# Two chained mixtures of experts after a dynamic convolution: one-hot rows built one group ahead, logits' steps with precedence in the order, and late second-layer weights for experts 4 to 7

## The chip, the cores and the metric

One core of one Trainium2 chip runs the whole program in one launch. The metric is the device time in microseconds (us). The engines are called as in the profile: PE (TensorE) multiplies matrices, PEld is its loading of stationary operands, DVE (VectorE) and ACT (ScalarE) work on whole tiles, POOL (GpSimd) issues the indirect transfers that gather and scatter rows, and SP (SyncE) issues all other DMAs and transposes from one queue. "The clock" is the TensorE clock that was granted, as a share of full speed: 1.00 is 2.4 GHz, 0.50 is 1.2 GHz.

## The reference

```python
# 7168 tokens of 192 numbers; 8 heads, 7 taps
w   = softmax(weight_gen, axis=-1)                       # per token and head
x   = einsum('bshk,bskhg->bshg', w, shifted(x_pad))      # dynamic convolution
# layer 1: 8 experts, 192 -> 1024 -> 192, two of them per token
l   = x @ w_gate + log1p(exp(x @ w_noise)) * noise
x   = sum over the 2 best experts e of l:  p_e * (relu(x @ w1[e]) @ w2[e])
# layer 2: 8 experts of the same size, one of them per token
l   = x @ w_gate2
x   = softmax(l)[best] * (relu(x @ w1b[best]) @ w2b[best])
```

What matters here is that a token's second-layer expert is known only when its first-layer output is complete, and that the rows must be sorted by expert before the big products start.

## The kernel before, in words

**Work and stages.** Tokens are handled in columns of 128, 56 columns in all. The first layer treats the columns in two groups: group 1 (columns j 0 to 17 of each half of the sequence) and group 2 (j 18 to 27). The products with the experts run in five phases, one after the other: phase 0 and phase 1 are the first layer on the early and the late columns of group 1, phase 2 is the first layer on group 2, phase 3 the second layer on group 1's tokens, and phase 4 the second layer on group 2's tokens. In a phase the sorted rows are cut into blocks of 128 rows with one expert each; two blocks with one expert make a double unit, else a block is a single unit. The first units of a phase have a fixed expert and read its weights from the resident tile `wres`; the singles that follow them may have any expert, and a copy `w` of the expert's weights is fetched for each of them by a DMA from SP, by ACT or by DVE (tuple `FE`, line 29).

**Products.** Weights and hidden values are kept as two f16 parts. `ph` is the first product of an expert, `hh` the rounded relu of it (ACT), `hl` the remainder (DVE, 128x512), `py` the second product. A step of a unit is ten matmuls of 256 columns (double) or twenty of 128 columns (single) into `ph`, followed by `py` matmuls of the unit before. Below, positions in a phase are counted in **pieces**: one piece is ten `ph` matmuls, so a step of a double unit is one piece and a step of a single unit two. A phase has 88 to 112 pieces; by count from the program's start, phase 3 holds pieces 288 to 376 and phase 4 pieces 376 to 464.

**A route** (`route_`, from line 1001) stands at the door of every phase. It is a chain: the logits of the last rows (`turn_thread`, line 647, has SP transpose the rows to `xtg`; `logit_thread`, line 668, multiplies them with the gate weights into `pm` and DVE writes `lg`), the choice of expert (`choose` or `settle`), ranks and places on DVE (`msk`, `blkh` and more), then one-hot rows on DVE in groups of `OG` = 8 columns (line 74): a one-hot of the place in the block (`pex`, from a comparison of `ipx` with the places) and one of the block (`bex`, comparison and multiplication by a code). PE multiplies each group's `pex` with `bex` into `pr` (lines 1191 to 1205), and from the sum DVE makes the table `src`. With `src`, POOL gathers rows (`gt<-rows,src`, `load_x`, line 1412), SP transposes them (`xt<-gt`, `turn_x`, line 1426) and `ph` of the next phase can begin.

**Between the layers.** POOL scatters first-layer outputs to `ybuf`. `combine_lane` (line 867) reads the two outputs of a token back (`rows<-ybuf`, `yl<-ybuf`, both on SP), sums them with the gates, splits the sum (`split_rows`), stores it (`store`, SP: `rows<-rows`) and puts it into the queue of `turn_thread`. `weight_lane` (line 463) loads raw weights of an expert and one of its two matrices (SP: `w<-in_moe_w_dram`; k=0 is the first matrix, k=1 the second), splits them on ACT and DVE and puts them into `wres`; for the second layer it starts with phase 2 (`replace_weights`, line 1551), and a matrix is written over the first layer's as soon as the last unit that needs the old one has been issued (`passed`).

**What sets the order.** All of this is written as Python generators, and the order of instructions on every engine is fixed when the program is built. `Feed` (line 211) holds the generators. Each says by `yield` on which engine its next instructions stand and which tiles they need (`yield None`: not now); `Clock` estimates when these would be ready. `pump`, called between the steps of the main loop (from line 1655), takes again and again the generator with the least time plus its `late` number, among those that are ready when PE would be free, so a lower `late` is a precedence. At a phase boundary whose route is not done, the rest of the route is issued without regard to PE (`until`). The second transpose of a four-column item, the logits and a `finish` thread (the end of a convolution item, started in `conv_lane`, line 762) are each such steps.

Each instruction is recorded from one helper, so all rows of the profile show one line, L189 (in the changed program L191).

```python
            for a in range(0, n, TPN):                 # turn_thread, TPN = 2
                ...
                xt = rt.tile([P, 4 * TPN, P], F16, name="xtg", bufs=XR)[:, 0:4 * k]
                yield "S", rows, xt
                SP.dma_start_transpose(xt, ...)
```

Of the kernel before, what the change touches and what calls it, by code (L numbers as in the profile page):

```python
# [16 lines left out]
P = 128  # L17
# [22 lines left out]
NC2 = 3  # L40
C2LATE = 0.0
R2LATE = -4.0
LLATE = 0.0
RLATE = -4.0
R0LATE = 2.0
XB = 1
TAPS = (2, 2, 2, 1)
# [2 lines left out]
HM = 1  # L50
WL2 = 2.0
EB = 2
TPN = 2
XR = 3
HT = 2
# [216 lines left out]
def moe_kernel(ctx: ExitStack, tc: tile.TileContext, x: bass.AP, wgen: bass.AP,  # L272
# [4 lines left out]
    V, A, G, PE, SP = [Eng(e, k, clk) for e, k in (  # L277
        (nc.vector, "V"), (nc.scalar, "A"), (nc.gpsimd, "G"), (nc.tensor, "P"), (nc.sync, "S"))]
    feed = Feed(clk)
# [8 lines left out]
    B, S, _ = x.shape  # L288
# [109 lines left out]
    wdone = [0, 0]  # L398
    have = [[[], []], [[], []]]
    started, pe_users, hurried = [], [], []  # L400
    passed = set()
    inv12 = [const.tile([P, E], F32, name=f"inv12_{m}") for m in range(2)]

# [59 lines left out]
    def weight_lane(m, tag, pieces, ln):  # L463
# [3 lines left out]
        def queue_of():  # L467

            return ("G", G) if m == 0 and not started and GQ else ("S", SP)

        def load(e, k):
            raw = wbuf.tile([P, 2 * QW], F16, name=tag, bufs=2).bitcast(F32)
            while m == 0 and (not loaded or hurried and not started):
                yield None
            q = queue_of()
            yield q[0], raw
            q = q[1]
            if k == 0:
                q.dma_start(raw[:, 0:F], wa[e, 0:P, :])
                q.dma_start(raw[0:64, F:QW], wa[e, P:D, 0:F // 2])  # L480
                q.dma_start(raw[64:P, F:QW], wa[e, P:D, F // 2:F])
            else:
                q.dma_start(raw.rearrange("p (f d) -> p f d", f=FT), wb[e].rearrange("(f p) d -> p f d", p=P))
            return raw
# [162 lines left out]
    def turn_thread():  # L647

        while True:
            if not queue:  # L650
                yield None
                continue
            r, ln, rows, t0, n = queue.pop(0)
            xts = []
            for a in range(0, n, TPN):
                k = min(TPN, n - a)
                while len(turned) >= XR:
                    yield None
                turned.append(1)
                xt = rt.tile([P, 4 * TPN, P], F16, name="xtg", bufs=XR)[:, 0:4 * k]  # L660
                yield "S", rows, xt
                SP.dma_start_transpose(xt, rows.bitcast(F16)[:, a:a + k].rearrange("p t c -> p (t c)"))
                xts += [xt[:, 4 * v:4 * v + 4] for v in range(k)]
            pending[ln] = False
            lqueue.append((r, t0, n, xts))
            yield ()
# [95 lines left out]
    def conv_lane(items, early, pool, ln):  # L762
# [39 lines left out]
        busy = []  # L802
        while cur:
# [56 lines left out]
            if q and (XB == 1 or ln):  # L860
                nxt = yield from load(*q)
            busy.append(1)
            feed.add(finish(r, acc, t0, n, busy, on_pe + (ln > 0), t), lane_th[ln][2])
            cur = q


    def combine_lane(r, pool, ln, idxs):
# [4 lines left out]
        while idxs:  # L872
# [9 lines left out]
            for c, o in ((1, z), (0, y)):  # L882
                k = 0
                while k < n:
                    t, v = at[b, ja + k], 1
                    while k + v < n and at[b, ja + k + v] == t + v:
                        v += 1
                    SP.dma_start(o[:, k:k + v], bass.AP(tensor=yb.tensor, offset=yb.offset + (2 * t + c) * P * D,
                                                        ap=[[D, P], [2 * P * D, v], [1, D]]))
                    k += v  # L890
            yield "A", z
            for v in range(n):
                A.activation(z[:, v], z[:, v], AF.Copy, scale=ga[:, at[b, ja + v], 1:2])
# [107 lines left out]
    def route_(r):  # L1001
# [186 lines left out]
            cin.at = at  # L1188

        extra = carried() if cin else iter(())  # L1190
        for k, (reg, c0, n) in enumerate(groups):
            lo = c0 % 16
            oh = rt.tile([P, P, OG], F16, name="pex", bufs=EB)[:, :, 0:n]
            ob = rt.tile([P, nblkm, OG], F16, name="bex", bufs=EB)[:, 0:nb, 0:n]
            yield "V", oh, ob
            next(extra, None)
            V.tensor_tensor(oh, ipx[:, :, 0:n], pos[:, None, c0:c0 + n].to_broadcast([P, P, n]), op=ALU.is_equal)
            next(extra, None)
            V.tensor_tensor(ob, ipx[:, 0:nb, 0:n], blk_[:, None, c0:c0 + n].to_broadcast([P, nb, n]), op=ALU.is_equal)
            next(extra, None)  # L1200
            V.tensor_tensor(ob, ob, code[:, None, lo:lo + n].to_broadcast([P, nb, n]), op=ALU.mult)
            yield "P", oh, ob
            for v in range(n):
                PE.matmul(tp[:, reg * nb:(reg + 1) * nb], oh[:, :, v], ob[:, :, v],
                          start=(lo + v == 0), stop=(lo + v == 15 or c0 + v == nw - 1))
        for _ in extra:
            yield "V",
        if cin:
# [170 lines left out]
    rts = [new_route(ph, gps[0, ph.g]) for ph in phases[:3]]  # L1379
    feed.add(first_loads(), -9.0)  # L1380
    feed.add(first_soft(), -1.0)
    logit_ths = [feed.add(turn_thread(), LLATE), feed.add(logit_thread(), LLATE)]
    items = [(r, i) for r in rts for i in range(r.n)]
    early = [(r, i) for r, i in items if r is rts[0] or r is rts[1] and i < BPE]
    for k in range(2):
# [16 lines left out]
    started.append(1)  # L1402
    for th in w_th:
        th[2] = PLATE
    feed.until(lambda: not pe_users and not pending[1] and lane_th[1] not in feed.threads)
    first_ths = [th for th in feed.threads if th not in logit_ths]
    raw.release()
# [342 lines left out]
```

## Time and profile before

| | |
|---|---|
| device time, 3 runs | 1026.44, 1036.34, 1036.35 us; median 1036.34 us |
| the profiled execution | 1031.08 us, its span 1029.3 us (1.8 us lie around the span) |
| PE, share of the span | 86% |
| DVE, share of the span | 72% |
| mean granted clock | 0.936 |

A row of the timeline gives the start in us from the span's start, the duration in us, the engine, the operation with what it writes and reads, how many instructions of that kind follow one another, and in brackets the idle time of the engine before it with what ended it. Work on different engines runs side by side, so a busy share below 100% is no loss by itself; what counts is what the engine that bounds a stretch waits for.

### The profile page before, as it was taken

What the parts mean: (1) busy time and instruction counts of PE and PEld (TensorE: products, weight loads), DVE (VectorE), ACT (ScalarE), POOL (GpSimd) and SP (SyncE); (2) the same over time, 40 slices, a digit from 0 to 9 for tenths busy, and PEclk for the clock granted to TensorE, in tenths of its full rate; (3) what the DMA queues carried; (4) which work ended last, traced back from release to release, by engine and by line L of the source; (5) the groups of instructions that cost most, each with busy time, mean ns of one, the idle gap of its engine ahead of it and who ended that gap; (6) DMA issues with size and microseconds to landing.
All of it is one profiled execution on the core that took longest, in us unless ns stands there. A gap on an engine that the chain in (4) does not pass through costs nothing. (4 is left out here: it accounts for less than half of the span.)

```text
span 1029.3 us, 26213 instructions
## 1 busy us (share of the span) xinstructions
PE 885.5 (86%) x10130; PEld 816.2 (79%) x10130; DVE 741.6 (72%) x1818; ACT 500.9 (49%) x1003; POOL 424.5 (41%) x575
## 2 busy tenths in 40 slices
PE   1995369999995999999679999998399999999985
PEld 0553259989995899999579988998298998999985
DVE  7686859899985998958565767758686879355442
ACT  1343049674441544556255876865084733344332
POOL 3020044555525455533343444443145544465542
PEclk8897579999997999999889999999599999999998
DMA  9256089979843877644499999995289876563592
GB/s 286 54 137 150 0 164 261 220 191 177 188 87 77 155 146 168 172 103 134 118 159 254 261 232 236 245 254 98 59 183 198 194 149 200 112 121 87 176 255 82
DMA packets 246369, 168.30 MB, mean 164 GB/s; under 512 B 177564, under 2 KB 228079, under 8 KB 246236
## 3 DMA queue, kind: packets, MB, share of 16 engines
q1 hardware_dynamic: 227500, 121.68, 53.3%
q0 software_dynamic: 18736, 44.85, 18.0%
q8 instruction: 83, 1.36, 0.6%
q14 instruction: 50, 0.41, 0.2%
HBM read 74.46 MB, written 32.59 MB: 104 GB/s over the span
## 5 line engine op out<-in xcount | busy, mean ns | idle before, releaser
L189 ACT ACTIVATE hh<-ph 128x512 f16<-128x512 f32 x362 | 214.3, 594 | 344.6 <-PE ph L189 303.1
L189 PE MATMUL ph<-xt,wres 128*128 128x256 f16 (+1 forms) x3200 | 327.1, 255 | 31.1 <-DMA xt<-gt 19.6
L189 DVE SCALAR_TENSOR_TENSOR hl<-ph,hh 128x512 f16<-128x512 f32 x362 | 245.3, 685 | 136.7 <-ACT hh L189 132.2
L189 PEld LDWEIGHTS <-wres 128*128 128x128 f16 x3200 | 266.2, 100 | 53.1 <-issue 29.7
L189 PE MATMUL py<-wres,hh 128*128 128x192 f16 x2048 | 271.9, 246 | 4.7 <-ACT yo L189 4.6
L189 PEld LDWEIGHTS <-hh 128*128 128x128 f16 x2896 | 261.6, 98 | 13.8 <-issue 8.9
L189 POOL DMA_INDIRECT gt<-rows,src x181 | 195.4, 1079 | 155.3 <-DVE wmx L189 72.6
L189 PE MATMUL py<-wres,hl 128*128 128x192 f16 x1024 | 251.9, 246 | 0.0
L189 POOL DMA_INDIRECT ybuf<-yo,dest x120 | 131.7, 1097 | 275.9 <-ACT yo L189 261.6
L189 PE MATMUL ph<-xt,w 128*128 128x128 f16 (+1 forms) x1600 | 137.2, 240 | 22.1 <-DMA xt<-gt 9.3
L189 PEld LDWEIGHTS <-hl 128*128 128x128 f16 x1448 | 141.8, 98 | 0.0
L189 PEld LDWEIGHTS <-w 128*128 128x128 f16 x1600 | 116.7, 100 | 29.5 <-issue 8.5
L189 PE MATMUL py<-w,hh 128*128 128x192 f16 x848 | 113.8, 247 | 2.1 <-DMA w<-wres 2.0
L189 POOL DMA_INDIRECT out_dram<-yo,dest x61 | 62.4, 1022 | 122.6 <-ACT yo L189 71.8
L189 PE MATMUL py<-w,hl 128*128 128x192 f16 x424 | 104.8, 247 | 0.0
L189 PE MATMUL acc<-prod,identf 128*128 128x384 f32 x168 | 62.2, 529 | 13.4 <-DVE prod L189 9.6
L189 PEld LDWEIGHTS acc<-prod,identf 128*128 128x128 f32 x168 | 33.9, 207 | 35.7 <-DVE prod L189 11.0
L189 DVE COPY w<-wres 128x3072 f16 x53 | 51.5, 975 | 12.6 <-issue 6.0
L189 ACT ACTIVATE yo<-py 128x192 f32<-128x192 f32 x120 | 37.2, 327 | 35.9 <-PE py L189 17.3
L189 DVE SCALAR_TENSOR_TENSOR wres<-w,wsc,wres 128x1024 f16<-128x1024 f32 (+1 forms) x32 | 49.4, 1545 | 3.6 <-ACT wres L189 3.6
L189 ACT ACTIVATE wres<-w,wsc 128x1024 f16<-128x1024 f32 (+1 forms) x32 | 43.5, 1358 | 12.7 <-DVE wsc L189 9.2
L189 DVE TENSOR_TENSOR acc<-acc,tmp 128x768 f32<-128x768 f32 (+1 forms) x60 | 47.9, 798 | 2.1
(201 smaller groups left out, 827.7 us busy)
## 6 DMA issues: line engine op xcount, KB each, us to landing
w<-wres SPq DMA_DIRECT2D x23, 768.0 KB
rows<-rows SPq DMA_DIRECT2D x24, 512.0 KB
w<-in_moe_w_dram SPq DMA_DIRECT2D x14, 768.0 KB
w<-in_moe_w_dram SPq DMA_DIRECT2D x13, 512.0 KB
xs<-in_x_dram SPq DMA_DIRECT2D x6, 960.0 KB
rows<-ybuf SPq DMA_DIRECT2D x10, 384.0 KB
yl<-ybuf SPq DMA_DIRECT2D x10, 384.0 KB
wres<-wbt SPq DMA_DIRECT2D x56, 64.0 KB
```

The lines of the kernel that those rows point to most:

```text
L189: return fn(*args, **kw)
```

## The change

It has three parts, and the set of instructions stays the same; their order changes.

1. **One-hot rows.** In `route_` the one-hot rows of a group are written before the products of the group ahead of it: up to `EB` = 2 groups are made, then the oldest one's products are issued. The step that writes one-hot rows no longer names their buffers to the planner (`yield "V",`).
2. **Precedence.** `turn_thread` and `logit_thread` get `LLATE` = -2 once the first phase has started (0 before that, as until now), `finish` threads get `FLATE` = -2 from then on, where they had the `late` of their lane. The second transpose of an item is issued with the first, without a step of its own.
3. **Held weights.** `weight_lane` issues no load of a second-layer matrix of experts 4 to 7 (`HOLD` = 4) before `summed` is set, which happens when a group's last read of `ybuf` has been issued.

```diff
-LLATE = 0.0
+LLATE = -2.0
+FLATE = -2.0
+HOLD = 4
...
+    summed = []
...
             q = queue_of()
+            while m and e >= HOLD and not summed:
+                yield None
             yield q[0], raw
...
                 xt = rt.tile([P, 4 * TPN, P], F16, name="xtg", bufs=XR)[:, 0:4 * k]
-                yield "S", rows, xt
+                if not a or not started:
+                    yield "S", rows, xt
...
-            feed.add(finish(r, acc, t0, n, busy, on_pe + (ln > 0), t), lane_th[ln][2])
+            feed.add(finish(r, acc, t0, n, busy, on_pe + (ln > 0), t), FLATE if started else lane_th[ln][2])
...
                     k += v
+            if not idxs:
+                summed.append(1)
...
         extra = carried() if cin else iter(())
-        for k, (reg, c0, n) in enumerate(groups):
+        def sums(hot):
+
+            (reg, c0, n), oh, ob = hot
+            for v in range(n):
+                PE.matmul(tp[:, reg * nb:(reg + 1) * nb], oh[:, :, v], ob[:, :, v],
+                          start=(c0 % 16 + v == 0), stop=(c0 % 16 + v == 15 or c0 + v == nw - 1))
+
+
+        made = []
+        for reg, c0, n in groups:
             lo = c0 % 16
+            if len(made) == EB:
+                yield ("P",) + made[0][1:]
+                sums(made.pop(0))
...
-            yield "V", oh, ob
+            yield "V",
...
-            yield "P", oh, ob
-            for v in range(n):
-                PE.matmul(tp[:, reg * nb:(reg + 1) * nb], oh[:, :, v], ob[:, :, v],
-                          start=(lo + v == 0), stop=(lo + v == 15 or c0 + v == nw - 1))
+            made.append(((reg, c0, n), oh, ob))
+        while made:
+            yield ("P",) + made[0][1:]
+            sums(made.pop(0))
...
-    logit_ths = [feed.add(turn_thread(), LLATE), feed.add(logit_thread(), LLATE)]
+    logit_ths = [feed.add(turn_thread()), feed.add(logit_thread())]
...
+    for th in logit_ths:
+        th[2] = LLATE
```

**On SP, shortly before the door of phase 3**, before: the last rows of group 1 (`rows_10459` and `rows_10139`) are stored, and their transposes to `xtg` stand behind pieces of a raw weight (`w<-in_moe_w_dram`).

```order
L189 DMA rows_65<-rows_10459 128x4x256
L189 DMA rows_65<-rows_10139 128x4x256
L189 DMA wres<-wbt_11137 64x512 x4
L189 DMA_TRANSPOSE xt<-gt 128x4x128 x2
L189 DMA w_11226<-in_moe_w_dram 128x1024
L189 DMA w_11226<-in_moe_w_dram 64x512 x2
L189 DMA_TRANSPOSE xtg<-rows_10459 128x8x128 x2
L189 DMA_TRANSPOSE xt<-gt 128x4x128 x2
L189 DMA w_11371<-in_moe_w_dram 128x8x192
L189 DMA_TRANSPOSE xtg<-rows_10139 128x8x128
```

The same place now, where these rows are called `rows_10044` and `rows_10161`.

```order
L191 DMA rows_65<-rows_10044 128x4x256
L191 DMA_TRANSPOSE xtg<-rows_10044 128x8x128 x2
L191 DMA_TRANSPOSE xt<-gt 128x4x128 x2
L191 DMA rows_65<-rows_10161 128x4x256
L191 DMA_TRANSPOSE xtg<-rows_10161 128x8x128
L191 DMA_TRANSPOSE xt<-gt 128x4x128
L191 DMA_TRANSPOSE xtg<-rows_10161 128x8x128
L191 DMA w_10965<-in_moe_w_dram 128x8x192
L191 DMA wres<-wbt_11239 64x512 x4
L191 DMA_TRANSPOSE xt<-gt 128x4x128 x2
L191 DMA w_11278<-in_moe_w_dram 128x1024
```

The transposes of the last rows have moved ahead of the last two raw weights; both of those loads now stand behind them.

**On DVE, in the route of the second layer's group 1**, before: from the last table (`blkh`) on, only one-hot rows.

```order
L189 CAST blkh<-sli 128x36
L189 TENSOR_TENSOR pex<-ipx,posh 128x1024
L189 TENSOR_TENSOR bex<-ipx,blkh 128x344
L189 TENSOR_TENSOR bex<-bex,code 128x344
L189 TENSOR_TENSOR pex<-ipx,posh 128x1024
```

And now.

```order
L191 CAST blkh<-sli 128x36
L191 SCALAR_TENSOR_TENSOR hl<-ph,hh 128x512
L191 TENSOR_TENSOR pex<-ipx,posh 128x1024
L191 TENSOR_TENSOR bex<-ipx,blkh 128x344
L191 TENSOR_TENSOR bex<-bex,code 128x344
L191 SCALAR_TENSOR_TENSOR hl<-ph,hh 128x512
L191 TENSOR_TENSOR pex<-ipx,posh 128x1024
```

The one-hot rows have moved between the last steps of phase 2, whose `hl` now stand among them; before, they stood behind the last of these.

**On SP, in phase 3**, before: the last rows of group 2 are stored (`rows_12209`, `rows_12211`, `rows_12213`) and turned for the logits (`xtg`) among the transposes of phase 3's own blocks (`xt<-gt`, two rows per unit of two blocks).

```order
L189 DMA_TRANSPOSE xt<-gt 128x4x128 x3
L189 DMA rows_65<-rows_12209 128x2x256
L189 DMA_TRANSPOSE xtg<-rows_12209 128x8x128
L189 DMA_TRANSPOSE xt<-gt 128x4x128
L189 DMA rows_65<-rows_12211 128x4x256
L189 DMA rows_65<-rows_12213 128x4x256
L189 DMA_TRANSPOSE xt<-gt 128x4x128 x6
L189 DMA_TRANSPOSE xtg<-rows_12211 128x8x128 x2
L189 DMA_TRANSPOSE xtg<-rows_12213 128x8x128
```

And now (`rows_12279`, `rows_12281`, `rows_12283`).

```order
L191 DMA_TRANSPOSE xt<-gt 128x4x128 x3
L191 DMA rows_65<-rows_12279 128x2x256
L191 DMA_TRANSPOSE xt<-gt 128x4x128 x2
L191 DMA rows_65<-rows_12281 128x4x256
L191 DMA_TRANSPOSE xt<-gt 128x4x128 x2
L191 DMA rows_65<-rows_12283 128x4x256
L191 DMA_TRANSPOSE xt<-gt 128x4x128 x4
L191 DMA_TRANSPOSE xtg<-rows_12279 128x8x128
L191 DMA_TRANSPOSE xtg<-rows_12281 128x8x128 x2
L191 DMA_TRANSPOSE xt<-gt 128x4x128 x2
L191 DMA_TRANSPOSE xtg<-rows_12283 128x8x128 x2
```

The first of these transposes to `xtg` stood right behind its store; now eight transposes of phase 3's blocks lie between the two, and the other four to `xtg` follow it.

## Rows read from the trace of the kernel before

**Rows 1.** The page's first part: busy time of each engine, instructions.

```profile
PE 885.5 (86%) x10130; PEld 816.2 (79%) x10130; DVE 741.6 (72%) x1818; ACT 500.9 (49%) x1003; POOL 424.5 (41%) x575
```

**Rows 2.** Windows: stretch, us, PE, PEld, DVE, ACT, POOL busy, clock, DMA share, GB/s.

```profile
712.00:747.00 35.00, 14.33 (x152) 13.18 (x150) 23.86 (x103) 6.03 (x10) 8.11 (x12) 0.61 0.25 61
747.00:838.00 91.00, 88.73 (x1123) 84.44 (x1121) 69.81 (x181) 56.88 (x140) 45.00 (x56) 1.00 0.88 178
838.00:880.00 42.00, 38.22 (x565) 36.98 (x564) 35.59 (x127) 14.62 (x34) 19.74 (x27) 1.00 0.70 204
```

**Rows 3.** Timeline of PE at the doors of phases 1 and 2.

```profile
331.90 2.29 PE L189 MATMUL ph<-xt,wres 128*128 128x256 f16 x10 [10.73 <-DMA xt<-gt]
...
456.79 0.17 PE L189 MATMUL pm<-gwh,xtg 128*128 128x16 f16 x1
...
504.71 1.55 PE L189 MATMUL ph<-xt,w 128*128 128x128 f16 x13 [8.33 <-DMA xt<-gt]
```

**Rows 4.** Timeline of DVE at the doors of phases 1 and 2.

```profile
322.71 0.20 DVE L189 TENSOR_SCALAR src<-ra 128x88 int32<-128x88 f32 x1
...
491.88 0.20 DVE L189 TENSOR_SCALAR src<-ra 128x72 int32<-128x72 f32 x1 [0.17 <-DVE ra L189]
```

**Rows 5.** Timeline of PE before and at the door of phase 3.

```profile
684.59 1.25 PE L189 MATMUL ph<-xt,wres 128*128 128x256 f16 x10
...
705.27 0.17 PE L189 MATMUL pm<-gwh,xtg 128*128 128x8 f16 x1
...
729.16 0.87 PE L189 MATMUL pr<-bex,pex 128*128 128x43 f16 x8 [11.41 <-DVE bex L189]
...
742.24 2.29 PE L189 MATMUL ph<-xt,wres 128*128 128x128 f16 x20 [8.14 <-DMA xt<-gt]
```

**Rows 6.** Timeline of DVE at the door of phase 3.

```profile
705.96 0.31 DVE L189 TENSOR_SCALAR lg<-pm,ix,gwt 128x32 f32<-128x32 f32 x1 [0.85 <-PE pm L189]
...
711.11 0.68 DVE L189 SCALAR_TENSOR_TENSOR hl<-ph,hh 128x512 f16<-128x512 f32 x1
711.72 0.37 DVE L189 CAST msk<-oh 128x288 f16<-128x288 f32 x1
...
728.77 0.34 DVE L189 TENSOR_TENSOR bex<-bex,code 128x344 f16<-128x344 f16 x1
...
733.30 0.25 DVE L189 TENSOR_TENSOR bex<-bex,code 128x172 f16<-128x172 f16 x1
...
735.65 0.18 DVE L189 TENSOR_SCALAR src<-ra 128x29 int32<-128x29 f32 x1
```

**Rows 7.** Timeline of SP's queue before the door of phase 3.

```profile
693.91 0.54 SPq L189 DMA_DIRECT2D w<-in_moe_w_dram  x1
```

**Rows 8.** Timeline of PE at the door of phase 4.

```profile
838.32 0.17 PE L189 MATMUL pm<-gwh,xtg 128*128 128x8 f16 x1
...
851.13 1.29 PE L189 MATMUL ph<-xt,w 128*128 128x128 f16 x20 [1.60 <-DVE w L189]
...
858.01 0.80 PE L189 MATMUL pr<-bex,pex 128*128 128x42 f16 x8
...
875.22 1.29 PE L189 MATMUL ph<-xt,wres 128*128 128x128 f16 x20
878.47 0.33 PE L189 MATMUL py<-w,hh 128*128 128x192 f16 x2 [1.96 <-DMA w<-wres]
```

**Rows 9.** Timeline of DVE at the door of phase 4.

```profile
842.64 0.96 DVE L189 COPY w<-wres 128x3072 f16 x1 [0.42 <-issue]
843.52 0.23 DVE L189 CAST msk<-oh 128x160 f16<-128x160 f32 x1
...
867.83 0.19 DVE L189 TENSOR_SCALAR src<-ra 128x42 int32<-128x42 f32 x1 [0.20 <-DVE ra L189]
```

**Rows 10.** Timeline of SP's queue at the door of phase 4.

```profile
872.00 1.20 SPq L189 DMA_TRANSPOSE xt<-gt  x1
874.37 0.50 SPq L189 DMA_DIRECT2D w<-wres  x1
```

## The prediction

> **What bounds the kernel now.** I read the page first. PE is busy for 885.5 us [rows 1] of a span of 1029.3, so some 144 us are left in which it waits or starts up, and no other engine comes near. Its slices in the page showed dips at the start of the phases, so I went on to windows around one such door: in the 35 us from 712 to 747 PE is busy for 14.33 us only and the clock is 0.61, while in the following 91 us it is busy for 88.73 at a clock of 1.00 [rows 2]. Inside a phase PE bounds, then, and a better order of other engines' work brings nothing there; at the doors a chain through DVE, POOL and SP bounds. Next I read PE's timeline at each door for what ended its waits, then DVE's for where the chain starts and what stands in it.
>
> Door 1: PE waits 10.73 us for gathered rows, door 2: 8.33 us [rows 3]. Door 3: 11.41 us for the one-hot rows and then 8.14 us for gathered rows, so 19.55 [rows 5]. Door 4 has no such wait: the chain's `src` is written at 867.83, the first product starts at 875.22 with no idle time ahead of it [rows 8, 9], and PE is busy for 38.22 of 42 us [rows 2]. There the chain just fits under PE's work. What the change can win is at doors 1 to 3, at most 10.73 + 8.33 + 19.55 = 38.6 us; what it can lose is mostly at door 4.
>
> **The change part by part.** The order tells which instruction stands ahead of which, the trace how long each takes. The set of instructions is the same, so nothing is added to the 885.5 us of PE or to DVE's 741.6 [rows 1].
>
> *Doors 1 and 2.* At door 1, DVE's order now has one step of the convolution (about 4.8 us of sums, by adding DVE's rows there) and two `hl` of 0.68 [rows 6] less ahead of `src`: 6 us, so `src` comes at 317 instead of 322.71 [rows 4], and PE's wait of 10.73 falls to about 5. At door 2 PE arrives 6 us earlier, but the last logits of group 2 (456.79 [rows 3]) stand four pieces later in PE's order, and the last three products of the route only at the end of the phase. Four pieces are about 9 us, less the 6 gained; so `src` comes near 493 instead of 491.88 [rows 4], and most of what door 1 gave is waited out here. I take +2 us for the two doors together (positive is a gain). Ends: +14 if door 2's chain does not move and both waits halve, -4.4 if door 1's 6 us are filled by other work of DVE and the four pieces count in part.
>
> *Door 3.* SP turns the last rows of group 1 ahead of two raw weights, and PE now has their logits behind piece 271, not 283. The trace's row for that piece is at 684.59; the logits ran at 705.27 [rows 5]. The chain from there: `lg` 0.7 later and, as in the trace, 5.8 from `lg` to `msk` (705.96 to 711.72 [rows 6]): 691.0. From `msk` to the end of the first one-hot group the trace takes 729.11 - 711.72 = 17.4. Now phase 2 still runs alongside, so seven more `hl` stand in that stretch, 7 x 0.68 = 4.8: 713.2. The last group ends 4.4 later (729.11 to 733.55), with two `hl` more 5.8: 719.0. Then 2.3 to the end of `src` (735.83), with one `hl` 3.0: 722.0. From `src` to the first product 742.24 - 735.83 = 6.4 [rows 5, 6]: 728.4. That is 13.8 us earlier than 742.24. Ends: 0 if the chain waits as long for something not seen here, and 19.55 if all of PE's waiting goes. A wait of some 7 us stays: PE's work of phase 2 ends at 729.16 - 11.41 = 717.8, and the products of the one-hots fill 3.5 of the 10.6 up to 728.4. So the half clock after this door stays too, and I count nothing for it.
>
> *Door 4.* Here the same precedence works backwards. The transposes of group 2's last rows now stand behind further `xt`, the reads of `ybuf` stand behind the last raw weights, and PE has the last logits at piece 358, not 348 of the program. In the trace the work that ends at 852.4 (851.13 + 1.29 [rows 8]) lies ahead of that place, so the logits come 14.1 us later than 838.32. The chain behind them takes 867.83 - 838.32 = 29.5 to `src`, less a copy of weights of 0.96 and an `hl` of 0.68 that no longer stand in it [rows 6, 9]: 27.9. With 0.2 for `src` and 6.6 to the first product this gives 852.4 + 34.7 = 887.1, against 875.22: 11.9 us lost. What hid the chain's 36.9 us was the work of 28 pieces; 18 are left. Ends: 0 if DVE, which is busy for 35.59 of 42 us there [rows 2], finds 12 us less other work in the chain, 14.1 if nothing shrinks.
>
> Two smaller terms lie at the same door. The copy of weights that PE awaits for 1.96 us at 878.47 [rows 8] is issued by SP at 874.37, behind the transpose at 872.00 [rows 10]; in the new order the weights stand ahead of that transpose: +2.0 (0 to 2.0). A new wait of 4 to 6 us at a door without one lets the clock fall: at door 3 a step of twenty matmuls takes 2.29 us behind the wait [rows 5], at full clock 1.29 [rows 8], and the slow stretch after such a wait is two to three steps: -2.3 (0 to -5).
>
> *Held weights.* The last raw weight is loaded at 693.91 [rows 7]; in the new order it keeps its place among the transposes of phase 2, and the last splits move from piece 290 to 300. Expert 7 is needed at piece 316. Phase 3's 88 pieces run from 742.24 to 875.22 [rows 5, 8], 1.5 us each, so 16 pieces leave 24 us: I count 0. A rule speaks against holding loads back: the Trainium skill, "DMA: Bandwidth & Descriptors", section "Rules for kernel authors", says to issue a DMA early and to wait late, so that its fixed cost lies beside work. By it the hold can only lose, which is rival C; the row at 693.91 shows no load here that is close to its use.
>
> *One-hot rows a group ahead.* By itself this lets DVE run on while PE multiplies. At door 3 PE waits only 0.40 between its products [rows 5], DVE being the slower of the two; I count 0 (0 to 1 us a door).
>
> The sum: 2 + 13.8 - 11.9 + 2.0 - 2.3 = 3.6 us. Against the profiled execution, 1031.08 us, that is 1027.5. The median of the runs is 1036.34, 5.3 above it, which gives 1032.7; the runs spread over 9.9 us around the profiled one, so I name the middle of the case, about 1031. Less or more than 1%, 10.4 us, is about what a measurement of this kernel can tell from no change.
>
> **The rivals.** *Main case: the wait moves from door 3 to door 4* (0.50), 3.6 us faster, within 1%. Its own range is -8 to +10 us of gain, 1021 to 1039.
>
> *A: door 4 holds* (0.27). The delay at door 4 is small, because the chain there contains waits that disappear when logits come later. For it: DVE's busy share there of 85% leaves other work that can slip behind the chain. Against it: 29.5 us of chain are mostly DVE's own rows. The rest is 2 + 13.8 + 2.0 = 17.8; with 4 us left at door 4 the gain is 13.8, so 1017 against the profiled execution, 1022 against the median. It decides where door 4 costs under 7.4 us.
>
> *B: slower* (0.18). The late logits of group 2 lose at two doors what group 1's win: -4.4 at doors 1 and 2, half of door 3 (7), the whole loss at door 4: -4.4 + 7 - 11.9 + 2.0 - 2.3 = -9.6, so 1041 and 1046. For it: the four pieces at door 2 and ten at door 4 are certain from the order, and the 13.8 rest on a chain in which DVE is never stopped. Against it: door 3's wait is the longest, and its logits are surely earlier. Beyond 10.4 us it needs the gains at doors 1 to 3 to stay under 2.
>
> *C: held weights come too late* (0.05). Experts 4 to 7 wait in phase 3; it takes a delay of more than the 24 us above, and each further 1.5 us of delay costs a piece. At 34 us it would cost 10 and give 1031.08 - 3.6 + 10 = 1037.5.
>
> **How the numbers follow.** Faster by over 1%: A's 0.27 and a tenth of the main case, 0.32. Slower by over 1%: two thirds of B, half of C and a little of the main case: 0.17. Within 1%: 0.51. The range reaches from A with nothing lost at door 4 (1031.08 - 17.8 = 1013, a little below) to B against the middle of the runs, 1044.
>
> **What would show it.** Right: after door 3's change the last `lg` of that route lies some 20 us ahead of the end of phase 2, PE waits under 10 us in all there, and the first product of phase 4 has a new wait of 5 us or more in front of it, for one-hot rows or for gathered rows. Wrong: a last `lg` of group 2 in phase 3 that comes no later than before, measured from the start of phase 3; a wait of PE on `wres` in phase 3 (C); a wait over 15 us at door 3; or a wait at door 2 that is longer than 12 us (B).

## The result, and the profile after

The changed kernel takes 1045.42 us (median of 7 runs, 1040.72 to 1047.48); the kernel before took 1030.76 us (7 runs) beside it. The ratio is 1.0126, 95% interval 1.0094 to 1.0157: slower by about 13 us, which is clear of no change but under 2%. The two medians are 14.7 us apart. A later measurement (h0, below) gave 1.0150 (1.0101 to 1.0200). The profiled execution of the changed kernel took 1045.78 us, 14.7 more than that of the kernel before. Single executions of one kernel differ by 7 us and more, so a stretch of a trace tells of one execution; the ratios tell of the kernel.

The busy time of the engines is nearly what it was [rows 1], with PE 7.0 us up; the page's first part after:

```profile
PE 892.5 (85%) x10130; PEld 821.4 (79%) x10130; DVE 742.3 (71%) x1818; ACT 498.9 (48%) x1003; POOL 430.7 (41%) x575
```

So the 14.7 us lie in waits and in the clock behind them. PE's timeline at the four doors and inside phase 2, after:

```profile
333.68 2.29 PE L191 MATMUL ph<-xt,wres 128*128 128x256 f16 x10 [10.97 <-DMA xt<-gt]
...
504.18 0.18 PE L191 MATMUL pr<-ge,ones 16*128 16x32 f16 x1 [4.28 <-DVE ge L191]
510.27 4.03 PE L191 MATMUL ph<-xt,w 128*128 128x128 f16 x40 [5.91 <-DMA xt<-gt]
519.11 2.31 PE L191 MATMUL ph<-xt,w 128*128 128x128 f16 x20 [4.81 <-DVE w L191]
...
617.72 1.25 PE L191 MATMUL ph<-xt,wres 128*128 128x256 f16 x10 [3.55 <-DMA xt<-gt]
621.78 0.18 PE L191 MATMUL pm<-gwh,xtg 128*128 128x8 f16 x1 [1.82 <-DMA xtg<-rows]
...
688.53 0.19 PE L191 MATMUL pm<-gwh,xtg 128*128 128x8 f16 x1 [3.42 <-DMA xtg<-rows]
...
727.85 0.83 PE L191 MATMUL pr<-bex,pex 128*128 128x43 f16 x8 [0.77 <-DVE bex L191]
...
746.84 2.31 PE L191 MATMUL ph<-xt,wres 128*128 128x128 f16 x20 [8.60 <-DMA xt<-gt]
...
872.80 0.80 PE L191 MATMUL pr<-bex,pex 128*128 128x42 f16 x8 [0.75 <-DVE bex L191]
...
889.87 2.32 PE L191 MATMUL ph<-xt,wres 128*128 128x128 f16 x20 [7.91 <-DMA xt<-gt]
```

Door 1's wait stayed (10.97 against 10.73 [rows 3]), door 2's grew from 8.33 to 4.28 + 5.91 with a further wait of 4.81 for a copy of weights, door 3's fell from 19.55 [rows 5] to 8.60, with 0.77 ahead of its one-hot products, and door 4, which had none [rows 8], waits 7.91. DVE's timeline, the chains behind these doors:

```profile
319.99 0.20 DVE L191 TENSOR_SCALAR src<-ra 128x88 int32<-128x88 f32 x1
...
469.36 0.34 DVE L191 TENSOR_SCALAR lg<-pm,ix,gwt 128x64 f32<-128x64 f32 x1
...
501.83 0.20 DVE L191 TENSOR_SCALAR src<-ra 128x72 int32<-128x72 f32 x1 [0.17 <-DMA ybuf<-yo,dest]
...
703.61 0.30 DVE L191 TENSOR_SCALAR lg<-pm,ix,gwt 128x32 f32<-128x32 f32 x1
707.06 0.30 DVE L191 CAST msk<-oh 128x288 f16<-128x288 f32 x1
...
727.46 0.34 DVE L191 TENSOR_TENSOR bex<-bex,code 128x344 f16<-128x344 f16 x1
...
737.68 0.18 DVE L191 TENSOR_SCALAR src<-ra 128x29 int32<-128x29 f32 x1
...
854.02 0.31 DVE L191 TENSOR_SCALAR lg<-pm,ix,gwt 128x32 f32<-128x32 f32 x1 [1.28 <-PE pm L191]
858.24 0.23 DVE L191 CAST msk<-oh 128x160 f16<-128x160 f32 x1
...
872.42 0.33 DVE L191 TENSOR_TENSOR bex<-bex,code 128x336 f16<-128x336 f16 x1
...
882.25 0.19 DVE L191 TENSOR_SCALAR src<-ra 128x42 int32<-128x42 f32 x1 [0.20 <-DVE ra L191]
```

The chain of door 4 takes 28.2 us from `lg` to `src`, about as long as before (28.8, from `lg` at 839.00 to 867.83 [rows 9]), but it starts 15.0 us later.

To compare kernels I cut each trace by pieces, from the start of one first-layer product to that of another (counted on PE's timeline; in us). By this count the phases start at pieces 0, 96, 176, 288 and 376, and the last ends at 480. The first column is phase 0 but for its last four pieces, the second holds phase 1 and doors 1 and 2, the third is phase 2 from its ninth piece on, the fourth door 3, the fifth phase 3, the sixth door 4. All traces of this table are from chips on which the kernel before takes about 1030 us.

| kernel | 0-92 | 92-184 | 184-287 | 287-292 | 292-348 | 348-380 |
|---|---|---|---|---|---|---|
| before | 171.9 | 205.4 | 197.4 | 35.1 | 91.2 | 42.7 |
| changed | 175.0 | 211.1 | 206.1 | 20.3 | 88.5 | 56.7 |
| changed, again (h0) | 175.1 | 211.2 | 206.8 | 20.1 | 87.7 | 56.6 |
| one-hot part alone (h1) | 171.8 | 207.8 | 208.6 | 28.2 | 90.2 | 47.8 |
| precedence alone (h2) | 176.7 | 209.7 | 198.3 | 21.0 | 92.2 | 43.3 |
| hold, sums earlier (h3) | 171.7 | 202.6 | 199.6 | 26.3 | 101.8 | 43.5 |
| from phase 2 on (k1) | 171.8 | 203.7 | 202.6 | 21.2 | 89.0 | 43.9 |
| k1 and one-hot (k2) | 171.7 | 202.9 | 203.4 | 20.5 | 88.3 | 56.2 |
| k2, door 4 early (k3) | 170.8 | 201.6 | 195.6 | 22.1 | 109.5 | 40.3 |

Changed against before: +3.1, +5.7, +8.7, -14.8, -2.7, +14.0, and with 1.7 at the start and -0.9 at the end the 14.7 us of the span.

The cuts at 92 and 184 fall into the doors, where the two kernels wait at different pieces. With cuts at 96, the first product of phase 1, and at 192, where phase 2 first reads `wres`, the first three differences are +0.1, +3.9 and +13.5: nothing is lost up to phase 1, little at door 2, and nearly all that door 3 wins is lost inside phase 2 ahead of it.

### The profile page after: what moved, and what is told of

Its sections match the earlier page's. It is cut to its first block, busy times and chain, and to the rows that moved or that the text cites. A ratio compares the mean times of both kernels' runs of the same rounds, so it can differ in the third digit from the quotient of the medians.

```text
span 1044.0 us, 26220 instructions
## 1 busy us (share of the span) xinstructions
PE 892.5 (85%) x10130; PEld 821.4 (79%) x10130; DVE 742.3 (71%) x1818; ACT 498.9 (48%) x1003; POOL 430.7 (41%) x575
## 5 line engine op out<-in xcount | busy, mean ns | idle before, releaser
L191 PE MATMUL ph<-xt,wres 128*128 128x256 f16 (+1 forms) x3200 | 331.7, 257 | 43.8 <-DMA xt<-gt 31.4
L191 POOL DMA_INDIRECT ybuf<-yo,dest x120 | 135.3, 1127 | 288.7 <-ACT yo L191 266.9
L191 POOL DMA_INDIRECT gt<-rows,src x181 | 195.6, 1081 | 137.2 <-DVE wg L191 72.6
L191 PEld LDWEIGHTS <-w 128*128 128x128 f16 x1600 | 116.1, 100 | 32.3 <-DVE w L191 11.9
L191 POOL DMA_INDIRECT out_dram<-yo,dest x61 | 62.8, 1029 | 135.0 <-ACT yo L191 90.6
L191 PE MATMUL acc<-prod,identf 128*128 128x384 f32 x168 | 62.9, 533 | 14.3 <-DVE prod L191 10.6
L191 PEld LDWEIGHTS acc<-prod,identf 128*128 128x128 f32 x168 | 33.9, 207 | 36.9 <-DVE prod L191 12.0
L191 ACT ACTIVATE yo<-py 128x192 f32<-128x192 f32 x120 | 36.9, 327 | 31.9 <-PE py L191 21.8
L191 ACT ACTIVATE wres<-w,wsc 128x1024 f16<-128x1024 f32 (+1 forms) x32 | 43.5, 1360 | 11.1 <-DVE wsc L191 9.2
```

The source lines that it names most:

```text
L191: return fn(*args, **kw)
```

## The experiments

The theory on trial, called the theory of places in the expectations: the time follows from where the last logits of a route stand in PE's order, because the chain behind them has a fixed length. Here the place of the last logits is the piece behind which they stand. Rivals: the one-hot part costs or gains by itself, and the hold costs by itself. The first two groups ran on chips on which the kernel before takes about 1058 us; there only ratios, and stretches against the kernel before on such a chip, are compared.

**First group.** e1 puts the products back behind their one-hot group:

```diff
-            made.append(((reg, c0, n), oh, ob))
+            yield "P", oh, ob
+            for v in range(n):
+                PE.matmul(...)
```

> The changed kernel with the one-hot rows written and multiplied group by group as before; precedence and hold stay. In its order the last logits of group 2's second layer stand behind piece 347 of the program (358 in the changed kernel, 348 before) and nothing else that stands at a door moves by more than two pieces. Theory of places (the time follows where the last logits of a route stand on PE): the 12 us lost at door 4 come back, the losses at door 2 and in phase 2 stay: 1045.4 - 12 = 1033 us, 0 to 4 us above the kernel before. Rival, the one-hot order by itself (DVE runs ahead with one-hot rows, so that remainders and copies of weights come late wherever a route runs): all doors gain, 1025 to 1030. Rival, the hold: nothing comes back, 1045.

e2 drops the precedence of `finish` threads:

```diff
-            feed.add(finish(...), FLATE if started else lane_th[ln][2])
+            feed.add(finish(...), lane_th[ln][2])
```

> The changed kernel without the precedence of the finish threads alone. In its order the last logits stand behind piece 151 at door 2 (159 changed, 155 before), 283 at door 3 (271, 283) and 347 at door 4 (358, 348). Theory of places: door 2 gains up to the 8 us that PE waited there before, doors 3 and 4 are as before: 1023 to 1028 us. Rival, the one-hot order by itself costs: slower than before, 1033 to 1040, since it is still there. Rival, the hold costs: slower than before too.

e3 is the kernel before with the hold alone:

```diff
+            while m and e >= HOLD and not summed:
+                yield None
```

> The kernel before with the hold of second-layer weights of experts 4 to 7 alone. In its order the last logits stand behind piece 274 at door 3 (283 before), the others within two pieces of before. Theory of places: door 3 gains about 1 us a piece, 9 us, door 4 loses up to 2: 1022 to 1026 us. Rival, weights held back come late for their first use: slower than before, with a wait on wres in phase 3: 1033 to 1045.

e4 is the kernel before with `HOLD = 2`, `LLATE = -4.0` and the second transposes without a step.

> Precedence of logits -4 and second transposes without a step, finish threads as before, one-hot rows as before, weights held from expert 2 on. In its order the last logits stand behind piece 151 at door 2 (155 before), 262 at door 3 (283) and 336 at door 4 (348); the last weights are split at piece 316, where expert 7 is first needed. Theory of places: door 2 gains up to 8, door 3 most of its 19.5, door 4 nothing: 1003 to 1012 us. Rival, weights come late: waits on wres in phase 3 give back 10 us or more, 1015 to 1030.

Measured: e1 1.0058 (1.0016 to 1.0100), e2 1.0036 (0.9997 to 1.0075), e3 0.9970 (0.9941 to 1.0000), e4 1.0173 (1.0116 to 1.0229). At door 4 e1 is as the theory of places had it: the stretch is 43.4 us there (46.0 in the kernel before on such a chip). Its ratio lies a little above the 0 to 4 us that were expected. e2 missed, and its ratio lies where both its rivals had it: with the logits four pieces earlier at door 2, piece 92 to 184 takes 208.3 against 206.1, so nothing is won there. The first product of phase 2 waits 1.15 us in place of 7.87, but PE now waits ahead of it for a copy of weights. PE's timeline of e2:

```profile
514.20 0.48 PE L191 MATMUL py<-w,hh 128*128 128x192 f16 x2 [3.81 <-DMA w<-wres]
519.35 4.04 PE L191 MATMUL ph<-xt,w 128*128 128x128 f16 x40 [1.15 <-DVE w L191]
```

e3 gained 0.3%, with an interval that reaches 1, where 0.5 to 0.8 was forecast: 9.6 us at door 3 (34.7 to 25.1), but 3.7 are given back in phase 2 and 5.6 at door 4, where its last logits stand two pieces later. e4 went the way of its rival, and further than the rival's range. PE's timeline of e4 in phase 3:

```profile
777.97 1.97 PE L191 MATMUL ph<-xt,wres 128*128 128x128 f16 x17 [3.25 <-DMA wres<-wbt]
...
799.66 1.97 PE L191 MATMUL ph<-xt,wres 128*128 128x128 f16 x17 [4.56 <-DMA wres<-wbt]
...
815.17 0.19 PE L191 MATMUL pm<-gwh,xtg 128*128 128x8 f16 x1 [4.92 <-DMA xtg<-rows]
```

Weights that are held too long arrive after their first use, and with them SP's whole queue is late: phase 3 takes 135.0 us instead of 99.1. The rule that the prediction cited against the hold (the Trainium skill, "DMA: Bandwidth & Descriptors", "Rules for kernel authors": issue early, wait late) is borne out here, at a hold from expert 2 on. The same trace shows what is left of the wait at door 3 when `src` is early. POOL's and DVE's timelines of e4 there:

```profile
742.87 0.97 POOL L191 DMA_INDIRECT ybuf<-yo,dest  x1 [1.89 <-ACT yo L191]
744.14 0.98 POOL L191 DMA_INDIRECT gt<-rows,src  x1 [0.30 <-issue]
```

```profile
738.02 0.18 DVE L191 TENSOR_SCALAR src<-ra 128x29 int32<-128x29 f32 x1
```

`src` is there at 738.2, but the first gather stands behind the scatters of phase 2's last blocks, and the last of these waits for ACT's `yo`, made from PE's last products. In every trace 6.0 to 7.5 us pass at this door from the first gather to the first product.

**Second group.** f0 is the kernel before; f1 restores the step between the two transposes (`yield "S", rows, xt` without the condition); f2 is e3 with `HOLD = 3`, which moves no logits; f3 has `HOLD = 3`, `C2LATE = -2.0` and the second transposes without a step.

> The kernel before once more, for its profile beside the others on this chip. Every theory: a ratio of 1.00, with waits of PE of 8 to 11 us at doors 1 and 2, some 19 us at door 3 and none at door 4.

> The changed kernel with the step between the two transposes of an item restored; the rest stays. In its order the last logits stand behind piece 160 at door 2 (159 changed), 271 at door 3 (271) and 358 at door 4 (358). Theory that the second transposes, issued without a look at the planner, block SP's queue and cost the 6 to 9 us of phase 2: phase 2 from its ninth piece to its last takes 196 to 199 us again (206 in the changed kernel on the first chip), the ratio to before is 1.003 to 1.007. Rival, theory of places alone (phase 2's waits belong to the early logits of door 3 themselves): no change from the changed kernel, 1.010 to 1.015.

> The kernel before with weights held from expert 3 on; in its order the last logits stand where they stand in the kernel before (155, 283, 348), and the last weights are split at the same piece, 290. Theory of places: 0.997 to 1.003. Rival, holding loads back costs by itself: 1.005 or more, with a wait on wres in phase 3. Rival, holding loads back frees SP and the DMA engines and gains by itself: 0.995 or less.

> The kernel before with the second transposes issued without a step, weights held from expert 3 on and a precedence of -2 for the sums between the layers. In its order the last logits stand behind piece 151 at door 2 (155 before), 266 at door 3 (283) and 347 at door 4 (348); the last weights are split at piece 304 of 316. Theory of places: door 2 gains 1 to 2 us, as the kernel without precedence of the finish threads showed, door 3 some 15 us (its stretch from the last piece of phase 2 to the first of phase 3 falls from 30 to 15 us), door 4 nothing: 0.982 to 0.990. Rival, work taken early at door 3 is given back inside phase 2: 0.995 to 1.005.

Measured: f0 0.9996 (0.9964 to 1.0028), f1 1.0051 (1.0016 to 1.0086), f2 1.0036 (0.9995 to 1.0077), f3 0.9992 (0.9960 to 1.0024). f1's ratio is in the theory's band, but not for its reason: phase 2 takes 207.5 us against 201.9 in f0, so its 6 us did not come back. What it has less is at the start: up to piece 96 it takes 200.1 us, against 203.7 in f0; why is not shown. f2 is not told apart from before by its interval. f3 missed, and its ratio is that of its rival: door 3 takes 18.6 us instead of 34.7, the largest gain of all, and the pieces up to 184 (+5.0), phase 2 (+8.6) and phase 3 (+4.1) give it back.

**Third group**, where the kernel before takes 1030.52 us. h0 is the changed kernel, h1 the one-hot part alone, h2 the precedence alone, h3 the hold with `C2LATE = -1.0`, a precedence of the sums between the layers.

> The changed kernel once more, beside its parts on the same chip. Every theory: 1.009 to 1.016, with piece 92 to the start of phase 3 about as long as before (the gain at door 3 eaten by door 2 and by phase 2), and phase 3 from its fifth piece to the fifth of phase 4 longer by 8 to 14 us.

> The kernel before with the one-hot rows written a group ahead, nothing else. In its order the last logits stand behind piece 160 at door 2 (155 before), 278 at door 3 (283) and 350 at door 4 (348), and door 4's last one-hot products behind 370 (366). Theory of places: door 2 loses 5 us, door 3 gains 5 and gives back 3 in phase 2, door 4 loses 5: 1.005 to 1.010. Rival, writing one-hot rows a group ahead lets DVE run on and gains where PE waits for them (11 us at door 3): 0.992 to 0.999.

> The kernel before with the precedence of logits, finish threads and second transposes, nothing else. In its order the last logits stand behind piece 159 at door 2 (155 before), 272 at door 3 (283) and 347 at door 4 (348). Theory of places: door 2 and phase 0 lose 5 to 9 us, door 3 gains 14, of which phase 2 takes 5 to 9 back, door 4 stays: 1.000 to 1.006. Rival, the precedence is the part that loses at door 4: 1.008 or more, with a wait there.

> The kernel before with weights held from expert 4 on and a precedence of -1 for the sums between the layers. In its order the last logits stand behind piece 155 at door 2 (155 before), 276 at door 3 (283) and 342 at door 4 (348), and the last weights are split at piece 296 (290; expert 7 is needed at 316). Theory of places: door 3 gains 7 to 9 us and gives back 2 to 4 in phase 2, door 4 gains 0 to 4: 0.989 to 0.996. Rival, whatever is taken early is given back in full: 0.997 to 1.003.

Measured: h0 1.0150, h1 1.0083 (1.0053 to 1.0112), h2 1.0027 (0.9997 to 1.0056), h3 1.0091 (1.0055 to 1.0126). h1 and h2 came out in the ranges of the theory of places, with one correction: in h1 the largest loss is phase 2, 11.2 us (13.8 from piece 192) where 3 were expected; PE's waits for `xtg` ahead of logits, summed over its timeline, are 10.5 us there (5.3 before). h3 missed, beyond its rival; PE's, DVE's and SP's timelines of h3 show why:

```profile
772.39 1.97 PE L191 MATMUL ph<-xt,wres 128*128 128x128 f16 x17 [8.62 <-DMA wres<-wbt]
```

```profile
762.77 0.74 DVE L191 SCALAR_TENSOR_TENSOR wbt<-w,wsc,wbt 128x512 f16<-128x512 f32 x1
```

```profile
760.57 7.37 SPq L191 DMA_TRANSPOSE xt<-gt  x4
...
769.69 2.41 SPq L191 DMA_DIRECT2D wres<-wbt  x4
```

The weight was split by 763.5, about when PE began to wait for it, but its copy into `wres` stands behind the 132nd transpose of rows on SP and was issued six us later. In the changed kernel the same copy stands behind the 125th and PE does not wait.

**Fourth group**, the kernel before at 1030.47 us. k1 takes the precedence of logits and the second transposes only from phase 2 on, with `HOLD = 3`; `finish` threads and one-hot rows are as before:

```diff
+    summed, second_on = [], []
...
-                yield "S", rows, xt
+                if not a or not second_on:
+                    yield "S", rows, xt
...
         if pi == 2:
+            second_on.append(1)
+            for th in logit_ths:
+                th[2] = LLATE
```

k2 is k1 with `if len(made) == (EB if r.m else 1):` in the one-hot part, so that rows go ahead in the second layer's routes alone. k3 is k2 with `HOLD = 4`.

> The kernel before with the precedence of logits and second transposes only from phase 2 on, and weights held from expert 3 on. In its order the last logits stand behind piece 155 at door 2 (155 before), 271 at door 3 (283) and 347 at door 4 (348); weights are split as in the run of the precedence alone. Theory of places: the precedence alone without its losses at door 2 and in phase 0; phase 2 and door 3 together gain 4 to 13 us, the rest as before: 0.988 to 0.996. Rival, what is taken early at door 3 is given back in phase 2: 0.998 to 1.004.

> The kernel from phase 2 on, with one-hot rows written a group ahead in the two routes of the second layer. In its order only door 4 differs from the run beside it: last logits behind piece 358 (347), last products of one-hots behind 374 (368). Theory of places: door 4 costs 10 to 14 us, 1.000 to 1.008, and its stretch from piece 348 to 380 takes 54 to 58 us against 43. Rival, the place does not matter there: equal to the run beside it.

> The same as the second with weights held from expert 4 on in place of 3. In its order the last logits stand behind piece 269 at door 3 and 336 at door 4, and the last piece of a weight is written to wres behind the 132nd transpose of rows on SP, where the kernel with the precedence of the sums had it too and waited 8.6 us. Theory of places: door 4's stretch takes 40 to 44 us although the one-hot part is in; a wait on wres of 5 to 12 us in phase 3 takes the gain of door 3: 0.994 to 1.004. Rival, one-hot rows ahead cost at door 4 by themselves: a stretch of 50 us or more there.

Measured: k1 0.9906 (0.9871 to 0.9941), k2 1.0009 (0.9978 to 1.0040), k3 1.0063 (1.0032 to 1.0095). Windows from piece 348 to 380, first k1, then k2, then k3 (columns as in rows 2):

```profile
827.48:871.42 43.94, 39.16 (x563) 37.78 (x562) 34.07 (x120) 15.09 (x34) 19.47 (x28) 1.00 0.64 198
```

```profile
827.04:883.21 56.17, 42.65 (x604) 40.79 (x602) 36.23 (x137) 15.14 (x35) 19.27 (x28) 0.91 0.64 165
```

```profile
837.62:877.92 40.30, 37.51 (x546) 36.20 (x544) 23.25 (x60) 13.90 (x30) 18.69 (x27) 1.00 0.85 213
```

k1 and k2 have the same places up to door 4. There k2's last logits stand eleven pieces later, and its stretch is 12.2 us longer, at a mean clock of 0.91. k3 has k2's one-hot part with the logits at piece 336, and its stretch is the shortest, 40.3: it is the place, not the one-hot rows. All 17 traces bear this out. By the place of the last logits of group 2, the stretch takes 40.3 us at 336 (two traces), 43.5 at 342, 42.7 to 46.7 at 347 and 348 (eight), 47.8 and 51.6 at 350, and 54.9 to 56.7 at 358 (four). At 336, 347 and 350 there are kernels with the one-hot part and without it; at 358 all have it. Door 3's stretch follows the place in the same way, but only up to a point: 34.7 to 36.9 us at 283, 28.2 at 278, 26.3 at 276, 25.1 at 274, and 18.6 to 22.1 in all ten traces with places from 272 down to 262. The first product of phase 4 in k1 and in k2, from their PE timelines:

```profile
865.31 1.28 PE L191 MATMUL ph<-xt,wres 128*128 128x128 f16 x20
```

```profile
876.40 2.31 PE L191 MATMUL ph<-xt,wres 128*128 128x128 f16 x20 [7.94 <-DMA xt<-gt]
```

k3 pays in phase 3, and more than foreseen: its ratio lies above the range of the theory. The wait for `xtg` is the longer one, not that on `wres`. Its PE timeline:

```profile
764.70 0.19 PE L191 MATMUL pm<-gwh,xtg 128*128 128x8 f16 x1 [10.44 <-DMA xtg<-rows]
771.77 1.97 PE L191 MATMUL ph<-xt,wres 128*128 128x128 f16 x17 [3.65 <-DMA wres<-wbt]
```

k1 beats both kernels: about 1% under the kernel before, and 2.2 to 2.4% under the changed one by the two ratios. It wins 13.9 us at door 3 and gives 5.2 of them back in phase 2 (7.6 from piece 192).

## Why the prediction was wrong, step by step

The forecast was 3.6 us faster; it came out 14.7 slower in the profiled executions, and the measured median lies 1.4 us above the range. The likeliest case had the right picture of doors 3 and 4 and a wrong sum. Term by term, forecast against measured: doors 1 and 2 +2 against -4.0 (up to piece 192), door 3 +13.8 against +14.8, door 4 -12.2 against -14.0 with 2.7 won ahead of it; phase 2, which is not in the sum, -13.5; the two ends of the span -0.8. All three signs of being right came true (`lg` 34.6 us ahead of PE's last product of phase 2, waits of 9.37 us at door 3, 7.91 ahead of phase 4), for they watched doors 3 and 4 alone.

Rival B, at 1041 and 1046, gave the time in part by luck. Its 1046 rests on a median of three runs, 1036.34; from the median of seven, 1030.76, its loss of 9.6 us gives 1040.4. It also took half of door 3's gain away at the door, where all of it was won.

*Door 4, -11.9 + 2.0 - 2.3 = -12.2.* Right: 14.0 lost from piece 348 to 380, and 2.7 won ahead of it. The first product stands at 889.87 with a wait of 7.91; e1, k1, k2 and k3 show the price of the place. The wait of 1.96 us for a copy of weights is gone, as forecast.

*Door 3, +13.8.* The term is right at the door, 14.8. What failed is that nothing was taken off for phase 2. The step is "Inside a phase PE bounds, then, and a better order of other engines' work brings nothing there", with nothing added to PE's 885.5 us: a worse order costs there. From piece 192 to 287 the changed kernel takes 13.5 us more. Summed over PE's timeline, its waits there are 14.3 us against 6.5: 7.0 for `xtg` ahead of logits (5.3 before), 3.9 for gathered rows (0.7) and 2.7 for `hl` (none) are the larger ones. The other 5.7 us are longer busy time. Windows from piece 232 to 271, first of the kernel before, then of the changed kernel with two stretches out of it (columns as in rows 2):

```profile
608.14:684.59 76.45, 72.43 (x873) 68.65 (x872) 54.47 (x159) 57.66 (x113) 35.74 (x49) 1.00 1.15 250
```

```profile
617.72:702.42 84.70, 77.40 (x910) 71.80 (x911) 56.47 (x166) 57.66 (x110) 34.09 (x48) 0.94 1.06 234
623.00:628.00 5.00, 4.81 (x43) 4.05 (x44) 3.37 (x19) 1.65 (x4) 0.00 (x0) 0.66 0.64 133
688.00:693.00 5.00, 3.72 (x35) 2.77 (x36) 2.21 (x4) 0.60 (x1) 0.00 (x0) 0.50 1.05 272
```

Here 8.3 us are lost. PE waits for rows at 617.72, just ahead of this stretch, and for transposes of logits at 621.78 and again at 688.53. Behind these places the clock is 0.66 and 0.50, where the kernel before has 1.00 throughout. So a wait inside the phase is paid twice here, as a wait and as slow products; forty more of the short logit products stand in the stretch as well. h0 has the same loss, 8.2.

The wait at 617.72 itself is for rows, and SP's timeline shows what stands ahead of their transposes:

```profile
603.66 2.58 SPq L191 DMA_DIRECT2D w<-in_moe_w_dram  x4
606.28 0.59 SPq L191 DMA_DIRECT2D rows<-ybuf  x1
606.91 0.51 SPq L191 DMA_DIRECT2D yl<-ybuf  x1
607.53 4.58 SPq L191 DMA_TRANSPOSE xt<-gt  x2
```

Four pieces of a raw weight and two reads of `ybuf` go first, and PE starts 10.2 us after SP turns to the transposes. Whether these are what made them late was not tried.

Which part of the change makes the 13.5 us is left open. From 192 to 287 the one-hot part alone loses 13.8 (h1), the precedence alone 5.9 (h2), k1 and k2 7.6 and 7.2. But e1, without the one-hot part, loses 15.7 against f0, and k3, with all three parts from phase 2 on, but for the precedence of `finish` threads and the one-hot part in the first layer, loses nothing (0.7 less than before). So it is argued, not shown, that the order which the planner makes of the parts costs this, and none of the parts as such.

*Doors 1 and 2, +2.* Wrong in size and sign. The step that failed is "PE's wait of 10.73 falls to about 5": it is 10.97. `src` did come earlier, at 319.99 instead of 322.71 [rows 4]. POOL's timeline of the changed kernel shows what was late next:

```profile
322.90 1.44 POOL L191 DMA_INDIRECT ybuf<-yo,dest  x1 [4.32 <-ACT yo L191]
...
324.65 0.97 POOL L191 DMA_INDIRECT ybuf<-yo,dest  x1 [0.22 <-issue]
325.92 0.98 POOL L191 DMA_INDIRECT gt<-rows,src  x1 [0.30 <-issue]
```

The gather stands behind scatters which wait for PE's own last products, as in e4. At doors 1 and 3 PE waits 8 to 11 us for gathered rows in every trace, however early `src` is. So PE does not reach door 2 six us earlier: the first product of phase 1 is 1.8 us later than before, as the first product of all is. The four pieces then delay the logits in full: `lg` is at 469.36, where it was at 457.48 before, 11.9 us later, and `src` is 9.95 later [rows 4]. Before, the first gather of this door stood at 496.16, behind a scatter and some 4 us behind `src`, so not all of the delay costs time: the first product of phase 2 is 5.6 us later than before, 3.8 of them lost here. The lower end given there, -4.4, is about what came, but it had the six us filled by other work of DVE.

Phase 0 was not in the sum, and costs nothing by piece 96 (194.1 us before, 194.2 changed, 194.1 in h0); h2, the precedence alone, takes 196.8.

*Held weights, 0.* Right for the changed kernel: no wait on `wres` in phase 3. That it was close is shown by h3, k3 and e4. *One-hot rows, 0.* Ahead of their group they cost nothing at door 4 when the logits stand early (k3), but the planner's order that came with them is not free: alone they cost 0.8% (h1).

## What to carry to other kernels

Price a door by where its chain's first instruction stands in the order of the engine that bounds, and count the chain's length against the work left behind that place: eleven pieces later cost 12.2 us here. Before a gain at a door is counted, look at what else stands in the queue ahead of the gather; a table that comes 3 us earlier won nothing because a scatter waited for the old work. A phase in which PE is the bound can still lose by a new order: here early logits whose rows were not there cost PE the wait and, behind it, products at a lower clock. Where a planner sets the order, each part moves places that it does not name, so try each part alone and limit it to the phase for which it is meant: the precedence of logits and second transposes, given only from phase 2 on and with a hold, is 1% faster than the kernel before.

## What the runs showed of the hardware

The kernel before took about 1058 us in the first two groups, which ran on two chips, and about 1030 in all other measurements. ACT's largest group of instructions was no slower; groups by line, first of the kernel before where it takes 1030 us, then of f0 (busy us and mean ns of one, then idle time before them by releaser):

```profile
L189 ACT ACTIVATE hh<-ph 128x512 f16<-128x512 f32 x362 | 214.3, 594 | 344.6 <-PE ph L189 303.1 <-issue 36.1 <-DVE hl L189 2.0
```

```profile
L189 ACT ACTIVATE hh<-ph 128x512 f16<-128x512 f32 x362 | 213.8, 594 | 376.4 <-PE ph L189 232.3 <-issue 61.9 <-remote 30.2
```

ACT waits 61.9 instead of 36.1 us for nothing that the profile shows, and 30.2 for something outside the core's engines. The doors take about as long on both kinds of chip (door 3: 35.1 and 34.7 us), the phases do not (phase 3: 91.2 and 99.1). What it is was not tried.
